# Attention with squared ReLU and a gated feed-forward on one core: swaps of normalised x two head pairs at a time, two loads moved up, the last tile's copies on VectorE

## The chip, the cores and the metric

The kernel runs on one core of a Trainium2 chip. The metric is the device time of one execution in microseconds (us). Before the change the median of six runs is 444.49 us, with 442.97 as the lowest and 447.28 as the highest.

## The reference

Attention over 8 batches, 12 heads, 448 positions and a head dimension of 64, whose scores go through a squared ReLU in place of a softmax; then, on the 3584 tokens of width 768, an RMS norm and a gated feed-forward of width 1536.

```python
scores = scale * np.matmul(q, k.transpose(0, 1, 3, 2))
attn = np.maximum(scores, 0.0) ** 2 / S
attn_out = np.matmul(attn, v)
x = attn_out.transpose(0, 2, 1, 3).reshape(B * S, H * D)
xn = x / np.sqrt(np.mean(x * x, axis=-1, keepdims=True) + 1e-06) * rms_g
g, val = xn @ w_gate, xn @ w_val
out = (g / (1 + np.exp(-g)) * val) @ w_out
```

## The kernel before

Two heads make a head pair, 128 rows of x transposed; a batch has six pairs (`HP` = `KT` = 6) and 448 columns. Everything runs in an order written out by hand: `weave(main, sides)` (line 17) interleaves a list of main units (feed-forward matmuls) with side steps (the attention of the next batch, loads, transposes), each side step having a position in the list. Each engine and each issuing queue works through its own instructions in that order.

Per batch b these stages follow each other:

- `fetch(b)` (line 88) loads q, k and v on POOL's queue, casting to bf16. Two buffers each hold the batches in turn.
- `trans_fill(b, half)` (line 677), for batches from 2 on: two DMA transposes on SP's queue (`transposes`, lines 163 and 167) make qT and kT of six heads, then two copies on POOL's queue (`fill`, lines 175 and 176) copy the halves of qT across the partitions. Batches 0 and 1 are transposed by TensorE instead (`pe_transposes`, line 128).
- Scores (lines 187, 207 and 228), ReLU on ScalarE or VectorE, squares on VectorE or ScalarE, the product with v (`attend`, line 273), and `leave` (line 288), which writes the pair's rows into xT on ScalarE.
- `norm_stat` (line 437) sums the squares over the rows on TensorE and takes the root and its reciprocal, `norm_spread` (line 476) spreads it over the partitions into rstd, and `norm_apply` (line 491) multiplies xT by it, pair by pair, on VectorE (line 500). For batches from 2 on it also issues the swaps.
- `swap` (line 339) makes xD, which is xT with its partition halves exchanged. Each swap is two DMAs on SP's queue (line 342), one for each half. It is needed because each matmul of the feed-forward uses 64 partitions: the upper half of the array multiplies by the gate weights, the lower by the value weights, and every head has to pass both.
- `gate_value(b)` (line 605): 12 blocks of 12 rounds each. A round (`rounds`, line 512) is one matmul for gate (psG) and one for value (psV) with one pair: six rounds over xT and six over xD, in order of the pairs. The order of the half blocks is such that the first two blocks' rounds over xT come before the first round over xD. Then silu on ScalarE (line 564) and the product into hT on VectorE (line 566).
- `out_tiles` (line 614): 128 tokens of two batches at a time, in a piece of 512 and a piece of 256 columns, each over the 12 row blocks of `wo_sb` (line 435). ScalarE copies the piece from PSUM (line 586), and `store` (line 592) issues the writes on SP's queue; those of the very last tile go on SP's and ScalarE's queues, and its second piece is cut in two of 128 columns.

At the start the loads stand on POOL's queue in the order q, k, v of batch 0, then slices of the gate and value weights with q, k and v of batch 1 between them, then six slices of w_out (`fetch_o`, line 117, each two row blocks of `wo_sb`), then q, k, v of batch 2 (line 743), then the fills of batch 2 (line 744). The attention of batch 0 is a list of units (`attention_first`, line 347), with pairs of matmuls on a constant tile between them (`warm`, line 656). Its end is written out (lines 707 to 738): single rounds of batch 0's feed-forward on x not yet normalised (`part`, line 703, the round numbers 0 to 5 over xT and 6 to 11, from `KT` on, over xD) are put between its last units and its norm. These first three blocks (psE) are copied out by ScalarE (`early_out`, line 532) and scaled later. SP's queue carries all the swaps, transposes and stores in one order.

Of the kernel before, what the change touches and what calls it, by code (L numbers as in the profile page):

```python
# [29 lines left out]
def along(p0, gap, fns):  # L30
    return [(p0 + gap * i, f) for i, f in enumerate(fns)]
# [3 lines left out]
def kernel(  # L35
# [11 lines left out]
    nc = tc.nc  # L47
    P = nc.NUM_PARTITIONS
    B, H, S, D = q.shape
# [4 lines left out]
    KT, FT, HP = DM // P, F // P, H // 2  # L54
# [3 lines left out]
    NT = 2 * S // P  # L58
# [20 lines left out]
    def head_rows(t, b, h0, h1):  # L79
        return t[b, h0:h1].rearrange("h (p c) d -> p h (c d)", c=NCH)  # L80
# [3 lines left out]
    def alloc_ld(b):  # L84
        for nm in ("q", "k", "v"):
            ld[nm, b] = ldpool.tile([PC, H, NCH * D], BF16, name=nm + "b", tag=nm + "b", bufs=2)

    def fetch(b):
        alloc_ld(b)
        for nm in ("q", "k", "v"):  # L90
            load(nm, b)

    def load(nm, b, h0=0, h1=H):
        src = {"q": q, "k": k, "v": v}[nm]
        return nc.gpsimd.dma_start(out=ld[nm, b][:, h0:h1, :], in_=head_rows(src, b, h0, h1))
# [13 lines left out]
    def fetch_gv(s):  # L109
        for prt, src in gv_slices(s * FS, (s + 1) * FS):  # L110
            last = nc.gpsimd.dma_start(out=wgv_sb[prt, :, s * FS : (s + 1) * FS], in_=src)
        return last

    def wo_rows(t, s):
        return t.rearrange("(fk p) m -> p fk m", p=P)[:, 2 * s : 2 * s + 2, :]

    def fetch_o(s):
        return nc.gpsimd.dma_start(out=wo_sb[:, 2 * s : 2 * s + 2, :], in_=wo_rows(moe_w_out, s))
# [37 lines left out]
    def transposes(b, half):  # L156

        hs = slice(half * HH, (half + 1) * HH)  # L160
        kT = late["kT"].tile([P, HH, 2, PC], BF16, name="kT", tag="kT")
        qT = late["kT"].tile([P, 3, HH, 2, PC], BF16, name="qT", tag="qT")
        nc.sync.dma_start_transpose(
            out=qT[:, 1].rearrange("p h c s -> p (h c) s"),
            in_=ld["q", b][:, hs, :].rearrange("p h m -> p (h m)"),
        )
        nc.sync.dma_start_transpose(
            out=kT[:].rearrange("p h c s -> p (h c) s"),
            in_=ld["k", b][:, hs, :].rearrange("p h m -> p (h m)"),
        )  # L170
        kqT[b, half] = (kT, qT)

    def fill(b, half, eng):
        qT = kqT[b, half][1]
        eng.dma_start(out=qT[:HALF, 2], in_=qT[HALF:, 1])  # L175
        eng.dma_start(out=qT[HALF:, 0], in_=qT[:HALF, 1])
# [156 lines left out]
    def cross(b, j, psAV):  # L333

        low, high = slice(0, HALF), slice(HALF, P)
        for to, fr in ((low, high), (high, low)):
            nc.scalar.mul(out=xDs[b][to, j, :], in_=psAV[fr, 0, :], mul=ga_sb[fr, j : j + 1])

    def swap(b, j0, j1, eng=None):

        for hf in (0, 1):
            (eng or nc.sync).dma_start(
                out=xDs[b][hf * HALF : (hf + 1) * HALF, j0:j1, :],
                in_=xTs[b][(1 - hf) * HALF : (2 - hf) * HALF, j0:j1, :],
            )
# [85 lines left out]
    def halves(ps, w, lhsT, rhs, start, stop):  # L431

        for hf in range(2):
            prt = slice(hf * HALF, (hf + 1) * HALF)
            nc.tensor.matmul(out=ps[prt, :w], lhsT=lhsT[:, prt], rhs=rhs, start=start, stop=stop)  # L435
# [55 lines left out]
    def norm_apply(b):  # L491


        raws = [xTs[b]] + ([xDs[b]] if b < 2 else [])
        if b == 0:
            xTs[b] = npool.tile([P, KT, S], BF16, name="xT", tag="xT", bufs=2)
            xDs[b] = npool.tile([P, KT, S], BF16, name="xD", tag="xD", bufs=2)
        for raw_x, x in zip(raws, (xTs[b], xDs[b])):
            for kt in range(KT):
                nc.vector.tensor_tensor(  # L500
                    out=x[:, kt, :], in0=raw_x[:, kt, :], in1=rstds[b][:], op=ALU.mult
                )
                if b > 1 and kt % 3 == 2:
                    swap(b, kt - 2, kt + 1)

    def hidden(b):
        i = b // 2
# [60 lines left out]
    osts = {}  # L568
# [8 lines left out]
    def out_piece(i, t, o, w):  # L577
        ps = ps_m.tile([P, 512], FP32, name="psO", tag="mm")
        for fk in range(FT):
            halves(  # L580
                ps, w, hTs[i][:, fk, t * P : (t + 1) * P], wo_sb[:, fk, o : o + w],
                fk == 0, fk == FT - 1,
            )
        if o == 0:
            osts[i, t] = late["ost"].tile([P, DM], FP32, name="ost", tag="ost")
        nc.scalar.copy(out=osts[i, t][:, o : o + w], in_=ps[:, :w])  # L586
        if (i, t) == (B // 2 - 1, NT - 1):
            store(i, t, o, o + w, (nc.sync, nc.scalar))
        elif o + w == DM:
            store(i, t, 0, DM, (nc.sync, nc.sync))  # L590

    def store(i, t, c0, c1, engs):
        g, end, k = t * P, (t + 1) * P, 0
        while g < end:
            n = min(end, (g // PC + 1) * PC) - g
            b, c, p0 = 2 * i + g // S, g % S // PC, g % PC
            c = c if b < 2 else (0, 2, 1, 3)[c]
            rows = out[b * S : (b + 1) * S, :].rearrange("(p u) m -> p u m", u=NCH)
            engs[k % 2].dma_start(
                out=rows[p0 : p0 + n, c, c0:c1],  # L600
                in_=osts[i, t][g - t * P : g - t * P + n, c0:c1],
            )
            g, k = g + n, k + 1
# [52 lines left out]
    def warm(n):  # L656

        ps = ps_m.tile([P, S], FP32, name="psW", tag="mm")
        for _ in range(n):
            nc.tensor.matmul(out=ps[:], lhsT=warm_in[:, :P], rhs=warm_in[:], start=True, stop=True)  # L660
# [8 lines left out]
    load("v", 1)  # L669
    for s in range(4, NSL):  # L670
        fetch_gv(s)
    for s in range(FT // 2):
        fetch_o(s)
    late["kT"] = pool("kT", 2)
    EB = 3
# [1 line left out]
    def trans_fill(b, half):  # L677
        transposes(b, half)
        fill(b, half, nc.gpsimd)

    with tc.tile_pool(name="qkT", bufs=2, side="right") as tp, tc.tile_pool(
        name="early", bufs=EB, side="right"
    ) as ep:
        late["qkT"], late["early"] = tp, ep
        warm(12)
        steps = attention_second(1)

        def early_block(fb):
            return [ps_m.tile([P, S], FP32, name="psE", tag="mm")[:] for _ in range(2)]

        units = attention_first(0)
        tail = len(units) - 4
        for n, fn in enumerate(units[:tail]):
            fn()
            if n % 3 == 2:
                warm(2)


        raw_x = xTs[0], xDs[0]
        psSS = ps_m.tile([P, S], FP32, name="psSS", tag="mm")  # L700
        blocks = [early_block(0)]

        def part(fb, *rs):
            for r in rs:
                rounds(0, fb, blocks[fb], r, r + 1, raw_x)

        psAV4 = psAVs[0, (HP - 2,)]
        squares_last, leave_4, attend_5, leave_5 = units[tail:]
        squares_last()
        part(0, 0, 1)  # L710
        pe_transposes(1, 0)
        leave_4()
        attend_5()
        leave_5()
        cross(0, HP - 2, psAV4)
        part(0, 2, 3, KT, HP - 2)
        norm_stat(0, psSS, steps.pop(0))
        part(0, KT + 1, KT + 2)
        norm_spread(0)
        blocks.append(early_block(1))  # L720
        part(1, *range(KT))
        part(0, HP - 1)
        part(1, *range(KT, KT + 3))
        part(0, KT + 4)
        steps.pop(0)()
        part(1, KT + 4)
        norm_apply(0)
        for fb in range(2):
            part(fb, KT + 3, KT + 5)
            early_out(0, fb, blocks[fb])  # L730
            if fb == 0:
                pe_transposes(1, 1)
        for fb in range(2, EB):
            blocks.append(early_block(fb))
            for r0 in range(0, 2 * KT, KT):
                steps.pop(0)()
                rounds(0, fb, blocks[fb], r0, r0 + KT, raw_x)
            early_out(0, fb, blocks[fb])
        main = gate_value(0, EB, KT // 2)
        sides = along(6.4, 2, [lambda fb=fb: early_scale(0, fb) for fb in range(EB)])  # L740
        sides += along(10.4, 2, [lambda fb=fb: early_rest(0, fb) for fb in range(EB)])
        sides += along(0, (len(main) - 1) / len(steps), steps[:-1])
        sides += [(18.2, lambda: fetch(2))]
        sides += [(28, lambda: trans_fill(2, 0))]
        weave(main, sides)
    late["ost"] = pool("ostage", 3)
    late["sum"] = pool("sum")
# [7 lines left out]
    for b in range(1, B):  # L755
# [5 lines left out]
        sides = []  # L761
# [39 lines left out]
```

## Time and profile before

| what | value |
|---|---|
| median of 6 runs | 444.49 us |
| the profiled execution | 445.35 us |
| its span, first to last instruction | 443.5 us |
| granted TensorE clock | 1.00 |
| mean data rate of the DMAs | 120 GB/s |
| packets of q0 (POOL's loads and fills) | 43.3% of 16 engines' span |
| packets of q1 (SP's queue) | 29.1% of 16 engines' span |

The span of the profiled execution lies within its time; what is in the time and not in the span are 1.9 us around it. A row of the page's fifth part has the line, the engine, the operation, what it writes and reads, the number of instructions, the busy time and the mean of one in ns, and then how long the engine sat idle before them. For the work around the change:

```profile
L242 ACT ACTIVATE r<-psS 112x896 bf16<-112x896 f32 x108 | 99.1, 918 | 22.2 <-PE psS L228 19.4
L435 PE MATMUL psO<-wo_sb,hT 128*64 128x512 bf16 (+2 forms) x1368 | 111.8, 323 | 0.0
L500 DVE TENSOR_TENSOR xT<-xT,rstd 128x448 bf16<-128x448 bf16 x48 | 26.4, 618 | 2.1 <-ACT rstd L488 2.1
```

And the DMA issues of the loads that move, with the size of one and the median time from issue to landing:

```profile
qb<-in_q_dram POOLq DMA_DIRECT2D x6, 672.0 KB, 12.2
kb<-in_k_dram POOLq DMA_DIRECT2D x6, 672.0 KB, 14.7
wo_sb<-in_moe_w_out_dram POOLq DMA_DIRECT2D x6, 384.0 KB, 16.3
xD<-xT SPq DMA_DIRECT2D x24, 168.0 KB, 2.7
```

In the timeline, one row is one instruction or several alike, with its start, its length, and in brackets how long its engine sat idle before it and what ended that. POOLq, SPq and ACTq are the queues' own instructions, such as DMA issues.

### The profile page before, as it was taken

Reading aid. Unit: us, or ns where it says so; the run is one execution under the profiler, and the core shown is the slowest. Engines: PE = TensorE matmul, PEld = TensorE weight load, DVE = VectorE, ACT = ScalarE, POOL = GpSimd, SP = SyncE. Lnnn points to the kernel's source line nnn. Section 1 sums busy time; section 2 is a strip of 40 time slices with the busy share of each in tenths; the row PEclk is TensorE's granted clock in tenths of the full one; section 3 lists DMA queues with packets and bytes.
Section 4 is the critical chain, followed back from the end, with each engine's and each line's share of the span. In section 5 each row is a group of like instructions: output and inputs, shape, how many; then the busy total and the mean of one; then the engine's idle time right before and its main releaser. Section 6 shows DMA issues by size and latency. Waiting matters only on the chain.

```text
span 443.5 us, 10907 instructions
## 1 busy us (share of the span) xinstructions
PE 433.3 (98%) x4720; PEld 249.5 (56%) x4720; DVE 287.7 (65%) x384; ACT 288.8 (65%) x448; POOL 53.7 (12%) x79
## 2 busy tenths in 40 slices
PE   7999999899999999999999999999999999999996
PEld 3345555655566545655566555665557555655664
DVE  4989985766853868666874668578676468742210
ACT  4899886577674775866755776666766667552221
POOL 8343300030000300021000300003000000000000
PEclk9999999999999999999999999999999999999999
DMA  9999999999216992179904997179912900041013
GB/s 130 196 201 198 200 215 193 150 198 171 58 37 133 192 167 57 37 179 168 148 18 111 190 201 81 35 121 185 170 37 68 227 7 1 1 120 51 1 37 109
DMA packets 86673, 53.21 MB, mean 120 GB/s; under 512 B 36577, under 2 KB 80737, under 8 KB 86625
## 3 DMA queue, kind: packets, MB, share of 16 engines
q0 software_dynamic: 44496, 27.50, 43.3%
q1 hardware_dynamic: 41504, 24.44, 29.1%
q8 instruction: 37, 0.61, 0.6%
q10 hardware_dynamic: 624, 0.57, 0.4%
q14 instruction: 12, 0.09, 0.1%
HBM read 47.19 MB, written 11.01 MB: 131 GB/s over the span
## 4 chain that ended last, share of the span: by engine, by line
PE 70%; DMA 19%; DVE 4%; ACT 2%; POOL 1%; issue 1%; SPq 0%; ACTq 0%; POOLq 0%
PE psG L520 26%; PE psO L435 18%; PE psV L520 13%; PE psAV L273 6%; PE psS L228 6%; DMA qb<-in_q_dram 4%; DMA kb<-in_k_dram 4%; DMA wgv_sb<-in_moe_w_gate_dram 4%; DMA qT<-qb 3%; DMA vb<-in_v_dram 2%; DVE xT L500 1%; DMA xD<-xT 1%; DVE r L240 1%; DMA qT<-qT 1%; DVE hT L566 1%
## 5 line engine op out<-in xcount | busy, mean ns | idle before, releaser
L520 PEld LDWEIGHTS <-wgv_sb 64*128 64x128 bf16 x2304 | 126.0, 94 | 96.1 <-issue 7.6
L520 PE MATMUL psG<-xT,wgv_sb 64*128 64x448 bf16 x558 | 128.7, 349 | 0.0
L520 PE MATMUL psV<-xD,wgv_sb 64*128 64x448 bf16 x558 | 128.4, 349 | 0.2 <-DMA xD<-xT 0.2
L520 PE MATMUL psG<-xD,wgv_sb 64*128 64x448 bf16 x558 | 128.4, 349 | 0.1
L520 PE MATMUL psV<-xT,wgv_sb 64*128 64x448 bf16 x558 | 128.0, 349 | 0.1
L242 ACT ACTIVATE r<-psS 112x896 bf16<-112x896 f32 x108 | 99.1, 918 | 22.2 <-PE psS L228 19.4
L435 PE MATMUL psO<-wo_sb,hT 128*64 128x512 bf16 (+2 forms) x1368 | 111.8, 323 | 0.0
L566 DVE TENSOR_TENSOR hT<-sil,psV 128x448 bf16<-128x448 bf16 x93 | 57.4, 617 | 62.7 <-ACT sil L564 62.6
L246 DVE TENSOR_TENSOR r<-r 112x1792 bf16<-112x1792 bf16 x72 | 78.0, 1088 | 30.8 <-ACT r L242 30.4
L435 PEld LDWEIGHTS <-hT 128*64 128x64 bf16 x1368 | 74.8, 110 | 35.7 <-issue 0.4
L564 ACT ACTIVATE sil<-psG 128x448 bf16<-128x448 f32 x93 | 50.5, 543 | 58.4 <-PE psV L520 34.6
L228 PE MATMUL psS<-qT,kT 64*128 64x448 bf16 (+1 forms) x288 | 57.1, 350 | 1.7 <-DMA qT<-qT 1.3
L586 ACT COPY ost<-psO 128x512 f32<-128x512 f32 (+2 forms) x57 | 26.2, 471 | 42.9 <-PE psO L435 42.5
L240 DVE TENSOR_SCALAR r<-psS 112x896 bf16<-112x896 f32 x36 | 39.0, 1084 | 2.0 <-PE psS L228 1.8
L273 PE MATMUL psAV<-r,vb 112*64 112x448 bf16 x384 | 40.3, 355 | 0.0
L175 POOL DMA_DIRECT2D qT<-qT x12 | 6.5, 541 | 264.7 <-PE psS L228 139.0
L273 PEld LDWEIGHTS <-vb 112*64 112x64 bf16 x384 | 20.1, 109 | 18.5 <-issue 6.5
L329 ACT ACTIVATE xT<-psAV,ga_sb 128x448 bf16<-128x448 f32 x47 | 27.8, 647 | 3.9 <-PE psAV L273 3.8
L228 PEld LDWEIGHTS <-kT 64*128 64x128 bf16 (+1 forms) x288 | 19.3, 97 | 16.1 <-issue 5.2
L500 DVE TENSOR_TENSOR xT<-xT,rstd 128x448 bf16<-128x448 bf16 x48 | 26.4, 618 | 2.1 <-ACT rstd L488 2.1
L471 DVE RECIPROCAL rhalf<-rhalf 128x224 f32<-128x224 f32 x8 | 12.4, 1553 | 21.3 <-ACT rhalf L465 21.3
L256 DVE TENSOR_TENSOR r<-r 112x1792 bf16<-112x1792 bf16 x23 | 24.3, 1083 | 0.7 <-ACT r L217 0.7
(67 smaller groups left out, 279.0 us busy)
## 6 DMA issues: line engine op xcount, KB each, us to landing
vb<-in_v_dram POOLq DMA_DIRECT2D x7, 672.0 KB, 18.7
qb<-in_q_dram POOLq DMA_DIRECT2D x6, 672.0 KB, 12.2
kb<-in_k_dram POOLq DMA_DIRECT2D x6, 672.0 KB, 14.7
qT<-qT POOLq DMA_DIRECT2D x24, 168.0 KB, 3.9
xD<-xT SPq DMA_DIRECT2D x24, 168.0 KB, 2.7
out_dram<-ost SPq DMA_DIRECT2D x7, 336.0 KB, 4.0
wgv_sb<-in_moe_w_gate_dram POOLq DMA_DIRECT2D x6, 384.0 KB, 16.3
wgv_sb<-in_moe_w_val_dram POOLq DMA_DIRECT2D x6, 384.0 KB, 16.7
```

The source lines that it names most:

```text
L228: nc.tensor.matmul(out=psS[: end - o, hf, :S], lhsT=flat[prt, o:end], rhs=qT[prt, 1 - hf : 3 - hf, h % HH], start=True, stop=True,)
L240: nc.vector.tensor_relu(out=r[:, cp], in_=src)
L242: nc.scalar.activation(out=r[:, cp], in_=src, func=ACT.Relu)
L246: nc.vector.tensor_tensor(out=r[:], in0=r[:], in1=r[:], op=ALU.mult)
L273: nc.tensor.matmul(out=part[hh * D : (hh + 1) * D, :], lhsT=ld["v", b][:, 2 * j + hh, c * D : (c + 1) * D], rhs=rsq[b, 2 * j + hh, c], sta ...
L329: nc.scalar.mul(out=xTs[b][:, j, :], in_=psAV[:, i, :], mul=ga_sb[:, j : j + 1])
L435: nc.tensor.matmul(out=ps[prt, :w], lhsT=lhsT[:, prt], rhs=rhs, start=start, stop=stop)
L500: nc.vector.tensor_tensor(out=x[:, kt, :], in0=raw_x[:, kt, :], in1=rstds[b][:], op=ALU.mult)
L520: nc.tensor.matmul(out=parts[part][:, :S], lhsT=wgv_sb[prt, h, fb * P : (fb + 1) * P], rhs=src[prt, kt, :], start=(r == 0), stop=(r == 2 * ...
L564: nc.scalar.activation(out=s[:], in_=psG, func=ACT.Silu)
L566: nc.vector.tensor_tensor(out=hT[:, fb, o : o + S], in0=s[:], in1=psV, op=ALU.mult)
L586: nc.scalar.copy(out=osts[i, t][:, o : o + w], in_=ps[:, :w])
```

## The change

Four edits:

1. In `norm_apply`, for batches from 2 on, the swaps are issued after every second pair instead of every third: three swaps (six DMAs of 112 KB) in place of two (four of 168 KB).
2. The copies of the very last output tile (pieces of 512, 128 and 128 columns) are done by VectorE instead of ScalarE. Their stores stay on SP's and ScalarE's queues.
3. Of the six slices of w_out only four stay ahead of the loads of batch 2. q and k of batch 2 follow them, then the other two slices, then the fills of half 0, then v. `trans_fill(2, 0)` stands at position 26 of the woven list instead of 28; on SP's queue this doesn't change the order.
4. At the end of batch 0's attention the last pair of warm-up matmuls is left out; rounds 2 and 3 move ahead of the transposes of batch 1, and rounds 7 and 8 (`KT + 1`, `KT + 2`) ahead of the norm's sums.

```diff
-                if b > 1 and kt % 3 == 2:
-                    swap(b, kt - 2, kt + 1)
+                if b > 1 and kt % 2:
+                    swap(b, kt - 1, kt + 1)
...
-        nc.scalar.copy(out=osts[i, t][:, o : o + w], in_=ps[:, :w])
-        if (i, t) == (B // 2 - 1, NT - 1):
+        last = (i, t) == (B // 2 - 1, NT - 1)
+        (nc.vector.tensor_copy if last else nc.scalar.copy)(
+            out=osts[i, t][:, o : o + w], in_=ps[:, :w]
+        )
+        if last:
             store(i, t, o, o + w, (nc.sync, nc.scalar))
...
-    for s in range(FT // 2):
+    for s in range(4):
         fetch_o(s)
...
         for n, fn in enumerate(units[:tail]):
             fn()
-            if n % 3 == 2:
+            if n % 3 == 2 and n < tail - 1:
                 warm(2)
...
         squares_last()
-        part(0, 0, 1)
+        part(0, *range(HP - 2))
         pe_transposes(1, 0)
...
         cross(0, HP - 2, psAV4)
-        part(0, 2, 3, KT, HP - 2)
+        part(0, KT, HP - 2, KT + 1, KT + 2)
         norm_stat(0, psSS, steps.pop(0))
-        part(0, KT + 1, KT + 2)
         norm_spread(0)
...
-        sides += [(18.2, lambda: fetch(2))]
-        sides += [(28, lambda: trans_fill(2, 0))]
+        sides += [(26, lambda: trans_fill(2, 0))]
+        alloc_ld(2)
+        load("q", 2)
+        load("k", 2)
+        for s in range(4, FT // 2):
+            fetch_o(s)
+        sides += [(26, lambda: load("v", 2))]
         weave(main, sides)
```

## The prediction

> **What bounds the kernel now.** I read the page's busy times first, then equal stretches of TensorE's work side by side, then the chain of waits where a stretch is longer than its twins.
>
> ```profile
> PE 433.3 (98%) x4720; PEld 249.5 (56%) x4720; DVE 287.7 (65%) x384; ACT 288.8 (65%) x448; POOL 53.7 (12%) x79
> ```
>
> TensorE is busy for 98% of the 443.5 us, at a granted clock of 1.00. An edit can thus take out a pause of TensorE, work of TensorE, or the start and end of the kernel; relief elsewhere is worth nothing. A busy TensorE may still issue late, so I compared stretches with the same 146 matmuls: from the first score of a batch's main stage (L228) to its first value product (L273), for batches 1, 2, 3 and 5. The first column is the stretch and its length, the next TensorE's busy time.
>
> ```profile
> 86.96:102.56 15.60, 14.31 (x146) 8.07 (x144) 11.28 (x15) 10.48 (x14) 3.90 (x5) 1.00 1.07 183
> 141.66:155.57 13.91, 13.91 (x146) 7.50 (x144) 9.58 (x11) 10.42 (x14) 3.91 (x5) 1.00 1.04 195
> 190.77:205.30 14.53, 14.41 (x146) 7.75 (x144) 9.58 (x11) 10.42 (x14) 3.90 (x5) 1.00 0.93 191
> 293.51:307.42 13.91, 13.91 (x146) 7.50 (x144) 9.58 (x11) 10.42 (x14) 3.90 (x5) 1.00 1.03 193
> ```
>
> 13.91 us is the undisturbed length (batches 4 and 6 have it too). Batch 1 loses 15.60 - 13.91 = 1.69 us, batch 3 loses 0.62. Batch 7 computes no scores; there one round stands 0.50 us from the one before where 0.19 is usual, which is 0.31 us, and with the unevenness behind it about 0.45. The cause in batch 1, from the timeline and the chain:
>
> ```profile
> 86.96 0.36 PE L228 MATMUL psS<-qT,kT 64*128 64x448 bf16 x1
> 88.61 0.35 PE L228 MATMUL psS<-qT,kT 64*128 64x448 bf16 x1 [1.29 <-DMA qT<-qT]
> ```
>
> ```profile
> 52.37 17.95 DMA qb<-in_q_dram
> ...
> 70.34 11.27 DMA qT<-qb
> ...
> 82.22 0.54 POOL qT L175
> 82.76 5.81 DMA qT<-qT
> ...
> 88.61 0.35 PE psS L228
> ```
>
> Four transfers in a row: load of q of batch 2, its transpose, the fill of the other half, and only then the second score matmul. In batch 3 the chain runs over the swap of normalised x:
>
> ```profile
> 187.43 3.31 DVE xT L500 x6
> 190.76 0.46 SPq L342
> 191.26 3.51 DMA xD<-xT
> 194.81 0.35 PE psV L520
> ```
>
> **The change, part by part.** All is deducted from the median of 444.49 us. The profiled execution took 445.35 us for a span of 443.5, so 1.9 us lie around the span; it is 0.86 above the median, so its stalls may be a little longer than usual.
>
> *Loads.* On POOL's queue the order becomes wo 0 to 3, q2, k2, wo 4 and 5, the two fills of half 0, v2; before it was wo 0 to 5, q2, k2, v2, fills. q2 moves up two places: from 52.37 to about the 48.43 at which wo 4 was issued. Two slices of wo are 768 KB; the transfers moved some 205 GB/s around 50 to 60 us, so q2 lands 3.8 us earlier, at 66.5. The transpose on SP's queue stands behind the swap of batch 1 that is issued at 67.04 for 1.10 us, so it starts at 68.2 instead of 70.34. With the old landing of 11.27 us it ends at 79.4, with the median of the qT transposes, 7.7, at 75.9. The fills then issue 0.6 and 1.15 us later, and with 5.81 (old) or 3.9 us (median) the second lands at 86.4 or 80.9. TensorE asks at 86.96. The 1.69 us go. k2 moves likewise, its transpose from 74.61 to about 70.8, so the swap behind it on SP (78.19 now, its xT ready at 76.0) comes sooner too. Bounds: nothing (the fill is as late as before) to 1.69. What is late next: wo 4 and 5, which now take the bytes' place of k2 and v2. As many bytes lie ahead of wo 5 as lay ahead of k2, which landed 20.2 us after 54.44, at 74.6:
>
> ```profile
> qb<-in_q_dram POOLq DMA_DIRECT2D x1, 672.0 KB, 18.0
> kb<-in_k_dram POOLq DMA_DIRECT2D x1, 672.0 KB, 20.2
> vb<-in_v_dram POOLq DMA_DIRECT2D x1, 672.0 KB, 23.7
> ```
>
> The first output tile starts at 74.59 and takes 2.59 us for its 12 rows of wo, so wo 5 (the last two) is wanted at 76.7. v2's tail beside the transposes shows what contention may add: 672 KB at 200 GB/s behind k2 would have landed at 78.0, and landed at 80.0. So wo 5 lands at 74.6 to 76.6: covered, barely. v2, now behind the fills on POOL, is issued at 77.5 to 81.1 and wanted at 102.56 - 1.69 = 100.9. Behind it on POOL wait the fills of half 1 (issued at 90.28) and the loads of batch 3; v2's issue costs them 0.95 us, and the half-1 fill is wanted only after the value product at 102.56.
>
> *Start of batch 0's tail.* One pair of warm-up matmuls goes (0.37 us of TensorE), two rounds (of 0.19 us) move ahead of the transposes and two ahead of the norm's sums. This gives nothing, because ScalarE sets the pace there: 7.88 and 8.00 us busy in the 8 us from 30 and from 38, and TensorE waits for it to empty a PSUM tile:
>
> ```profile
> 37.61 0.94 ACT L532 COPY gv<-psE 128x448 f32<-128x448 f32 x2
> 38.18 0.79 PE L520 MATMUL psE<-xT,wgv_sb 64*128 64x448 bf16 x3
> ```
>
> What TensorE saves before 38.18 it waits there. If that cover failed I would gain 0.37. The moved rounds read xD of pair 2, whose second swap is issued at 25.10; swaps there land in 5.8 to 6.1 us, so at 31.2, wanted at about 31.9. If it came late, the norm's sum (32.22 to 32.99) has 0.33 us before ScalarE takes it. Bounds 0 to 0.37 gain; taken 0.
>
> *Swaps in twos.* Six transfers of 112 KB instead of four of 168 KB in each of six norms. SP spends 0.46 to 0.60 us on each, so the first starts after two multiplies (188.58, not 189.16), and two still follow the last multiply at 190.74: at about 190.9 and 191.4, the latter 0.15 later than now. What TensorE stalled on, pair 3, leaves in the middle swap, issued 1 us earlier; pair 4 is wanted 0.19 us after it, at 194.38. Cautiously, the last swap lands after the old 3.51 us less 56 KB at the 237 GB/s of 191.2 to 193.2 (0.24 us): 194.68, a stall of 0.30 instead of 0.62. In batch 7 the same reckoning gives 396.26 + 2.81 - 0.24 = 398.83 against 398.67, a stall of 0.16 instead of 0.45. At best, since the data starts to move 0.6 us sooner, both stalls go: 1.07. At worst the size matters nothing and only the 0.19 of the later want counts, less 0.15: 0.04 a place, 0.1 in all. I take 0.8, between the cautious 0.6 and the best. The transposes queued behind on SP are delayed by the 0.15 us and have many us in hand; in batches 2, 4 and 6 the swaps are not waited for.
>
> The Trainium skill speaks against this edit: "DMA: Bandwidth & Descriptors", section on the anatomy of one DMA, puts about 2.0 us fixed on every transfer and only bytes / 436 GB/s on top, so that 112 KB would land merely 0.13 us before 168 KB; by that this part would be worth about 0.4 us. The rule is fitted on loads that GpSimd issues, the swaps leave SP. The trace, where 168 KB landed in 2.8 to 3.5 us, agrees with a large fixed share; it doesn't separate the two.
>
> *Last tile.* Its three copies go from ScalarE to VectorE, which is idle then.
>
> ```profile
> 439.51 0.38 ACTq L599 DMA_DIRECT2D out_dram<-ost  x1
> 439.93 0.27 ACT L586 COPY ost<-psO 128x128 f32<-128x128 f32 x1 [0.45 <-ACT ost L586]
> 440.30 0.33 ACTq L599 DMA_DIRECT2D out_dram<-ost  x1
> ```
>
> The last matmul starts at 439.21 and takes 0.22, but the copy waits until 439.93 for ScalarE, which is issuing a store. VectorE would start at 439.46. Its price for 128 f32 columns from PSUM isn't in the trace: 0.16 us by proportion from its 224-column f32 copy (282 ns), 0.40 by the line through its PSUM reads of 448 and 896 columns (684 and 1084 ns); I take 0.28, the nearest row. The store then issues at 439.79, not 440.30: 0.51 less (0.39 to 0.57, since ScalarE's queue is busy with the second store until about 439.7).
>
> Sum: 1.69 + 0 + 0.8 + 0.51 = 3.0 us; 444.49 - 3.0 = 441.5.
>
> **The rivals.** *The swaps in twos bring nothing* (0.1 instead of 0.8): 444.49 - 1.69 - 0.1 - 0.51 = 442.2. For it: the last swap starts no earlier. Against it: the late pair is no longer in the last swap. *The wait at 86.96 only moves*: wo 5 lands late at 76.7, or the fill does: 444.49 - 0.8 - 0.51 = 443.2. For it: the margins of 0.1 and 0.56 us at the far ends. Against it: the near ends leave 2 and 6 us. *Slower: v2 comes too late.* It moved from 56.34 to behind the fills; at the far end 81.1 plus the longest landing of a vb load, 23.7, is 104.8, a wait of 3.9 us at L273, so 444.49 - 3.0 + 3.9 = 445.4. It decides from a landing after 103.9. Against it: those 23.7 us stood behind two slices of wo, q2 and k2, and the shortest vb load took 7.6.
>
> **How the numbers follow.** Forecast 0.62 (440.8 to 442.2 with its own bounds), swaps nothing 0.14, the wait moves 0.15, slower 0.09. About 0.5%, 2.2 us, is what a measurement of this kernel can tell from no change: faster is below 442.27, slower above 446.71. Nine tenths of the forecast and half of the first rival are faster, 0.63; beyond 446.71 v2 must land after 106, past all rows, 0.07; the rest is the same, 0.30. The range runs from the forecast's best with TensorE's 0.37 (440.4) to the second rival with a late pair of wo (444.2), which leaves out the slower one.
>
> **What would show it.** Right: the stretch of batch 1 is 13.91 us long; no wait for qT or xD; transposes at 68; the last store issues at 439.8 less what came before; TensorE's pause at 38 grows by some 0.37. Wrong: an output tile at 76 that waits for wo, a first value product that waits for vb, a stretch of batch 3 still at 14.5, or ScalarE moving ahead before 38.

## The result, and the profile after

The changed kernel takes 443.21 us as the median of 33 runs (442.32 to 443.95), the kernel before 444.38 us as the median of its 70 runs now (442.74 to 448.16). The ratio is 0.9973, with a 95% interval of 0.9963 to 0.9983: 1.17 us faster, less than half of the 3.0 us forecast, and by the prediction's own bound of 0.5% no change. The time lies in the range (440.4 to 444.2). The runs also lie closer together: 8 in 10 of them between 442.67 and 443.81, before between 443.14 and 445.67.

The profiled execution took 442.98 us for a span of 441.2, at a granted clock of 1.00; before it was 445.35 us for 443.5. The two profiled executions thus differ by 2.4 us where the medians differ by 1.2, and a comparison of the two profiles alone would find twice the gain that the times show. Of the 2.4 us, 0.40 lie ahead of the first value product, at 13.01 us before and 12.61 after; in the thirteen traces read here it comes at 12.31 to 13.02 us, whatever the edit. First the busy times, from the first part of the page of the changed kernel:

```profile
PE 432.0 (98%) x4718; PEld 248.8 (56%) x4718; DVE 288.8 (65%) x387; ACT 287.6 (65%) x445; POOL 53.9 (12%) x79
```

Two matmuls and three ScalarE copies fewer, three VectorE copies more; the other instruction counts in this row are the same. Then the same stretches as in the prediction, from the first score to the first value product of batches 1, 2, 3 and 5 (columns: stretch and length, then TensorE's busy time and others):

```profile
86.43:100.41 13.98, 13.98 (x146) 7.49 (x145) 11.29 (x15) 10.40 (x14) 3.89 (x5) 1.00 1.01 187
139.50:153.42 13.92, 13.92 (x147) 7.52 (x145) 9.58 (x11) 10.42 (x14) 3.92 (x5) 1.00 1.08 211
188.61:203.26 14.65, 14.28 (x147) 7.71 (x146) 9.70 (x11) 10.40 (x14) 3.91 (x5) 1.00 0.85 179
291.48:305.39 13.91, 13.91 (x146) 7.51 (x144) 9.58 (x11) 10.42 (x14) 3.90 (x5) 1.00 0.95 186
```

Batch 1's stretch went from 15.60 to 13.98, the undisturbed length. Batch 3's did not get better: 14.65, against 14.53 before. In the timeline of the changed kernel the loads, fills, transposes and swaps in front of batch 1's stretch now stand as follows, first POOL's queue and then SP's (start, length, line, operation, and what ended the idle time before it):

```profile
48.21 0.96 POOL L95 DMA_DIRECT2D qb<-in_q_dram  x1 [1.60 <-ACT r L217]
50.17 0.94 POOL L95 DMA_DIRECT2D kb<-in_k_dram  x1 [1.01 <-DVE hT L566]
51.95 0.71 POOL L118 DMA_DIRECT2D wo_sb<-in_moe_w_out_dram  x1 [0.83 <-DMA wgv_sb<-in_moe_w_gate_dram]
54.94 0.71 POOL L118 DMA_DIRECT2D wo_sb<-in_moe_w_out_dram  x1 [2.28 <-DMA wgv_sb<-in_moe_w_val_dram]
75.54 0.56 POOL L175 DMA_DIRECT2D qT<-qT  x1 [19.89 <-DMA qT<-qb]
76.09 0.55 POOL L176 DMA_DIRECT2D qT<-qT  x1
76.62 0.99 POOL L95 DMA_DIRECT2D vb<-in_v_dram  x1
```

```profile
67.65 1.53 SPq L163 DMA_TRANSPOSE qT<-qb  x1
69.23 4.83 SPq L167 DMA_TRANSPOSE kT<-kb  x1
75.44 1.83 SPq L342 DMA_DIRECT2D xD<-xT  x2
```

q of batch 2 is issued at 48.21 instead of 52.37, its transpose starts at 67.65 instead of 70.34, and the fill is issued at 75.54, eleven microseconds before the first score. In the list of TensorE's waits there is none for qT any more; for the swaps there still is:

```profile
PE psV L520 <- DMA xD<-xT: 0.3, 1, 0.3
```

### The profile page after: what moved, and what is told of

It reads as the page before. It is cut to its first block, busy times and chain, and to the rows that moved or that the text cites. A ratio compares the mean times of both kernels' runs of the same rounds, so it can differ in the third digit from the quotient of the medians.

```text
span 441.2 us, 10928 instructions
## 1 busy us (share of the span) xinstructions
PE 432.0 (98%) x4718; PEld 248.8 (56%) x4718; DVE 288.8 (65%) x387; ACT 287.6 (65%) x445; POOL 53.9 (12%) x79
## 4 chain that ended last, share of the span: by engine, by line
PE 86%; ACT 7%; DVE 4%; issue 1%; DMA 1%; SPq 0%; ACTq 0%; DVEq 0%
PE psG L520 30%; PE psO L435 23%; PE psV L520 13%; PE psAV L273 9%; PE psS L228 6%; ACT r L217 2%; PE psW L663 2%; DVE r L240 1%; PE psS L187 1%; ACT r L197 1%; ACT sil L564 1%; DVE hT L566 1%; DMA xD<-xT 1%; DVE xT L500 1%; PE psT L143 1%
## 5 line engine op out<-in xcount | busy, mean ns | idle before, releaser
L228 PE MATMUL psS<-qT,kT 64*128 64x448 bf16 (+1 forms) x288 | 56.1, 350 | 0.4
L587 ACT COPY ost<-psO 128x512 f32<-128x512 f32 (+1 forms) x54 | 25.1, 477 | 39.8 <-PE psO L435 39.8
```

Source lines behind the costliest of these rows:

```text
L228: nc.tensor.matmul(out=psS[: end - o, hf, :S], lhsT=flat[prt, o:end], rhs=qT[prt, 1 - hf : 3 - hf, h % HH], start=True, stop=True,)
L587: (nc.vector.tensor_copy if last else nc.scalar.copy)(out=osts[i, t][:, o : o + w], in_=ps[:, :w])
```

## The experiments

All ratios are against the kernel before on the same chip. The runs came on three chips, whose medians of the kernel before were 443.86, 443.99 and 444.87 us; runs of one chip are compared with each other.

### Each edit by itself

First chip, four kernels: the kernel before with one edit of the change each. In the cuts of code, `...` stands for lines left out. The loads:

```diff
-    for s in range(FT // 2):
+    for s in range(4):
         fetch_o(s)
...
-        sides += [(18.2, lambda: fetch(2))]
-        sides += [(28, lambda: trans_fill(2, 0))]
+        sides += [(26, lambda: trans_fill(2, 0))]
+        alloc_ld(2)
+        load("q", 2)
...
+        sides += [(26, lambda: load("v", 2))]
```

> The kernel before with the new order of loads alone (edit 3). Theory A, the whole gain of 1.17 us comes from this edit: ratio to before near 0.9975 (1.0 to 1.3 us faster), narrower spread of times than before (before: 442.7 to 448.2), batch 1's stretch 13.9 to 14.0 us instead of 15.60. Rival B, this edit gives the full 1.69 us that the profiled execution of before lost and another edit gives 0.5 back: ratio near 0.9962.

The swaps:

```diff
-                if b > 1 and kt % 3 == 2:
-                    swap(b, kt - 2, kt + 1)
+                if b > 1 and kt % 2:
+                    swap(b, kt - 1, kt + 1)
```

> The kernel before with the swaps in twos alone (edit 1). Theory A, a swap lands some 3.4 us after its issue whatever its size, so nothing is won: ratio 0.999 to 1.001, batch 3's stretch still 14.5 to 14.7 us, batch 7 still with a wait of 0.1 to 0.5 us. Rival B, the two more issues cost time: ratio 1.001 or more. The prediction's own figure was 0.8 us faster, 0.9982.

The last tile:

```diff
+        last = (i, t) == (B // 2 - 1, NT - 1)
-        nc.scalar.copy(out=osts[i, t][:, o : o + w], in_=ps[:, :w])
+        (nc.vector.tensor_copy if last else nc.scalar.copy)(
+            out=osts[i, t][:, o : o + w], in_=ps[:, :w]
+        )
```

> The kernel before with the last tile's copies on VectorE alone (edit 2). Theory A, the copies are earlier but the stores, now back to back on two queues, take longer to issue (0.85 and 1.03 us for the second pair in the changed kernel instead of 0.37): 0.1 to 0.2 us faster, ratio 0.9996, the last store issued about 1.3 us after the last matmul's start. If the stretched issue was chance: 0.5 us faster, ratio 0.9989, the last store 0.6 us after. Rival B: slower, 1.0005 or more.

The start:

```diff
-            if n % 3 == 2:
+            if n % 3 == 2 and n < tail - 1:
                 warm(2)
...
-        part(0, 0, 1)
+        part(0, *range(HP - 2))
...
-        part(0, 2, 3, KT, HP - 2)
+        part(0, KT, HP - 2, KT + 1, KT + 2)
         norm_stat(0, psSS, steps.pop(0))
-        part(0, KT + 1, KT + 2)
```

> The kernel before without the last warm-up pair and with the rounds moved (edit 4). Theory A, ScalarE sets the pace at 28 to 38 us: ratio 0.9995 to 1.0005, and TensorE's first block after the pause at 38 starts at the same distance from ScalarE's copy. If TensorE's saving came through: 0.37 us faster, 0.9992. Rival B, this edit costs time: 1.0005 or more.

| edit alone | median us | ratio, 95% interval | profiled us |
|---|---|---|---|
| loads | 443.71 | 0.9984 [0.9963, 1.0005] | 443.78 |
| swaps | 444.66 | 1.0012 [0.9990, 1.0035] | 444.68 |
| last tile | 443.95 | 0.9996 [0.9980, 1.0012] | 444.61 |
| start | 444.91 | 1.0016 [0.9993, 1.0039] | 447.14 |

No interval excludes 1. By the ratio the loads bring 0.7 us (by the medians 0.15) and the others nothing that shows, so the times alone settle little here; the traces have to do it.

The loads do in the trace what was expected. From the value products ahead of the first output tile to the next ones, 29.51 us before (73.05 to 102.56), it is 27.90 with the loads alone and in six of the seven other traces with the new order that are read here; the seventh, with 28.59, is told below. With the old order it is never below 28.91.

The start edit's trace shows 39.35 us from the first value product (about 13 us) to the one at 52, as the traces of the loads, the swaps and the last tile alone do (39.35 or 39.36), and 39.51 before, 39.37 after. It is worth nothing that shows. Its long profiled time has another cause, and that is the old order of the loads at its worst. From the chain of waits of the kernel with the start edit alone (start, length, what; `...` stands for lines left out):

```profile
57.34 17.48 DMA qb<-in_q_dram
74.84 8.59 DMA qT<-qb
...
84.57 4.66 DMA qT<-qT
89.27 0.35 PE psS L228
```

q of batch 2 was issued at 57.34 there, 5 us later than in the trace of before, and the stretch from 73 took 30.60 us. The load's place in POOL's queue is the same in both. What held POOL isn't settled: it sits idle for some microseconds before each load, and the releaser named differs from run to run. Nor does the issue alone set the loss: with the swaps alone q of batch 2 was issued at 54.42 and 1.01 us were lost, before at 52.37 and 1.61, since there the transfers behind it took longer (transpose 11.27 us and second fill 5.81, against 10.87 and 4.57).

So the old order's loss varies from one execution to the next, and the traces of five kernels that have it show how (the loss is the stretch less 27.90; beside it, how far the profiled execution lies above the median of its kernel's runs):

| kernel with the old order | loss us | profiled less median us |
|---|---|---|
| swaps alone | 1.01 | 0.02 |
| before | 1.61 | 0.97 |
| changed, old loads (below) | 1.66 | 1.06 |
| last tile alone | 1.72 | 0.66 |
| start alone | 2.70 | 2.23 |

The execution that took the median time lost 1.0 us; the others lost more, and were longer by nearly as much. The five lie 1.0 us above their medians on average. In seven traces with the new order the profiled execution lies 0.5 us below to 0.8 us above, on average at the median; an eighth, told below, lay 1.2 above.

### The change less one edit, and two variants of it

Second chip. The changed kernel with swaps in threes again:

```diff
-                if b > 1 and kt % 2:
-                    swap(b, kt - 1, kt + 1)
+                if b > 1 and kt % 3 == 2:
+                    swap(b, kt - 2, kt + 1)
```

> The changed kernel with the swaps in threes again (edit 1 undone, edits 2 to 4 kept). Theory A, a swap in twos is worth only the 0.2 us that batch 7 showed: median within 0.3 us of the changed kernel's, batch 3's stretch 14.3 to 14.8 us, the last stage (first matmul of batch 7 to its first output matmul) 27.97 us instead of 27.80. Prediction's figure, 0.8 us for the swaps: about 0.8 us slower than the changed kernel.

The changed kernel with ScalarE's copies at the end again:

```diff
-        (nc.vector.tensor_copy if last else nc.scalar.copy)(
+        nc.scalar.copy(
```

> The changed kernel with the last tile's copies on ScalarE again (edit 2 undone). Theory A, the store issues set the end, and their length varies (0.38 to 1.12 us for the second one over four executions with ScalarE): 0.1 to 0.4 us slower than the changed kernel, last store issued 1.1 to 1.8 us after the start of the last matmul. Prediction's figure: 0.5 us slower.

The changed kernel with the last piece of 256 columns whole:

```diff
-        if (i, t, o) == (B // 2 - 1, NT - 1, 512):
-            for o, w in ((o, w // 2), (o + w // 2, w // 2)):
-                out_piece(i, t, o, w)
-            return
```

> The changed kernel with the last tile's second piece whole, 256 columns in one copy and two stores instead of two copies and four stores. Theory A, the second pair of stores holds up the third, so leaving it out brings the last store to about 0.7 us after the start of the last matmul (a copy of some 0.42 us after its 0.22) instead of 1.0 to 1.3: 0.3 to 0.6 us faster than the changed kernel, ratio to before near 0.9963. Rival, the end is set by the size of the last copy and the landing of a store: 0.1 us faster to 0.2 us slower than the changed kernel.

And a test of what the swaps' time hangs on. In batches 3, 5 and 7 the pairs 3 to 5 are swapped before the norm, as soon as their rows are in xT, and VectorE multiplies their xD as well; pairs 0 to 2 are swapped together after three multiplies, and the other batches' swaps go in threes:

```diff
             leave(b, (j, j + 1))
+            if b % 2 and j:
+                swap(b, max(j, 3), j + 2)
...
+        early_x = b > 1 and b % 2
+        if early_x:
+            raws.append(xDs[b])
...
+                if early_x:
+                    if n == 0 and kt == 2:
+                        swap(b, 0, 3)
+                elif b > 1 and kt % 3 == 2:
+                    swap(b, kt - 2, kt + 1)
```

> The changed kernel, but for batches 3, 5 and 7 the pairs 3 to 5 are swapped before the norm, and their xD is then multiplied on VectorE (three more multiplies of 0.62 us a batch); pairs 0 to 2 go in one swap after three multiplies; batches 2, 4 and 6 swap in threes. Theory A, what TensorE waits for is the time from a swap's issue to its landing, 2.3 to 3.6 us whatever its size, after the last multiplies: with those swaps out of the way batch 3's stretch falls from 14.65 to 13.9 us and the last stage from 27.80 to about 27.5: 0.7 to 1.0 us faster than the changed kernel. Rival, VectorE becomes the bound in these stages: the stretches of batches 3 and 5 grow beyond 14.0 and nothing is won.

| changed kernel with | median us | ratio, 95% interval | profiled us |
|---|---|---|---|
| swaps in threes | 443.65 | 0.9992 [0.9979, 1.0006] | 444.87 |
| ScalarE's copies | 443.65 | 0.9988 [0.9975, 1.0001] | 443.70 |
| last piece whole | 443.07 | 0.9976 [0.9964, 0.9988] | 442.54 |
| swaps before the norm | 442.67 | 0.9967 [0.9954, 0.9979] | 442.82 |

*Swaps.* In batch 3's stretch, undisturbed 13.91 us, five traces with swaps in threes show 14.32 to 15.31 (mean 14.80), and six with swaps in twos 14.45 to 14.74 (mean 14.62). From the first matmul of batch 7's feed-forward to the first of its output tiles, swaps in threes show 27.95 to 28.02 us and swaps in twos 27.72 to 27.81: 0.22 less. By the traces swaps in twos thus bring some 0.4 us in all: the 0.22 in batch 7, where the two groups lie apart, and 0.18 in batch 3, where they overlap. Why so little is in the chain of waits of the changed kernel around batch 3's norm:

```profile
185.91 2.67 DVE xT L500 x5
...
188.64 0.58 SPq L342
...
189.32 0.55 SPq L342
189.86 0.05 issue
189.92 3.35 DMA xD<-xT
193.27 0.04 issue
193.31 0.35 PE psV L520
```

The last of the six swaps carries 112 KB and lands 3.35 us after it is issued, at 193.27; before, 168 KB took 3.51. The multiplies end at 188.58 (185.91 + 2.67), so this last transfer is issued 1.34 us after them; before, with one pair of DMAs less, it was 0.52 (191.26 against 190.74). SP's queue is behind: the trace has its six issues at 186.47, 186.98, 188.10, 188.64, 189.32 and 189.92, and the third stands 0.59 us after its pairs were multiplied (187.51), in batch 5 only 0.17. What it waited for in batch 3 isn't settled, but it isn't chance: in all six traces with swaps in twos it is 0.57 to 0.59 us. The later ones have to queue behind it; even in batch 5 the last swap is issued 0.98 us after the multiplies' end. TensorE stops twice on the way, for the middle pairs and for the last ones (from the timeline):

```profile
191.84 0.35 PE L520 MATMUL psG<-xD,wgv_sb 64*128 64x448 bf16 x1
192.29 0.35 PE L520 MATMUL psV<-xD,wgv_sb 64*128 64x448 bf16 x1
...
192.69 0.35 PE L520 MATMUL psG<-xD,wgv_sb 64*128 64x448 bf16 x1
193.31 0.35 PE L520 MATMUL psV<-xD,wgv_sb 64*128 64x448 bf16 x1 [0.27 <-DMA xD<-xT]
```

A round usually follows the one before by 0.19 us, here by 0.45 and 0.62: 0.26 and 0.43 us lost, 0.69 of the 0.74.

The long landings go with something that the chain doesn't name. Among the DMA queues the page of the changed kernel lists one whose kind is "instruction":

```profile
q8 instruction: 37, 0.61, 0.5%
```

Each of its 37 packets carries 16 KB. The trace has their times: in batch 3 one runs from 189.86 to 190.95, while the last four swaps are under way; in batch 5, which doesn't stall, none runs while the swaps do. In the eleven traces whose swaps are all in twos or all in threes, batches 2 to 7, this parts the landings:

| swaps | no such packet in the first 2.6 us after the issue | with one |
|---|---|---|
| 112 KB | 152 landed after 2.12 to 2.44 us, median 2.23 | 64 after 2.17 to 4.19, median 3.33 |
| 168 KB | 83 landed after 2.53 to 3.09 us, median 2.61 | 37 after 2.51 to 4.38, median 3.42 |

So the smaller size lands some 0.4 us sooner, and a packet of q8 beside a swap goes with about 1 us more, whatever the size. That the packet delays the swap is read from this; no edit moved the packets, and whose instructions they carry isn't shown. In batch 7 no such packet runs beside the last swaps, and there the two effects of the edit can be seen bare: the last swap lands after 2.33 us instead of 2.81, and is issued 1.01 us after the last multiply instead of 0.53. They cancel. What is left is that the last swap now holds pairs 4 and 5, which are wanted 0.19 us later than pair 3.

With the swaps of three pairs before the norm, the same stretch and that of batch 5 are:

```profile
189.00:202.92 13.92, 13.92 (x147) 7.52 (x146) 11.16 (x14) 10.42 (x14) 3.88 (x5) 1.00 1.03 184
291.13:305.05 13.92, 13.92 (x148) 7.53 (x146) 11.16 (x15) 10.42 (x14) 3.89 (x5) 1.00 0.98 190
```

No wait for xD is left on TensorE's list, although VectorE has three multiplies more there (11.16 us busy instead of 9.70 in batch 3). In this trace the wait has thus gone. Two things differ at once, though: half of the pairs were swapped early, and batch 3's packet of q8 begins at 190.89, after the last swap has landed (190.68).

*Last tile.* VectorE's copies start when the matmuls end and the last one takes 0.29 us. But the stores don't follow. From the timeline of the changed kernel, the last matmuls, VectorE's last copy, and the second and third stores on ScalarE's queue (four views):

```profile
437.01 0.22 PE L435 MATMUL psO<-wo_sb,hT 128*64 128x128 bf16 x2
437.27 0.29 DVE L587 COPY ost<-psO 128x128 f32<-128x128 f32 x1 [0.38 <-PE psO L435]
437.18 1.03 ACTq L602 DMA_DIRECT2D out_dram<-ost  x1
438.30 0.39 ACTq L602 DMA_DIRECT2D out_dram<-ost  x1
```

The last copy ends at 437.56, and its store is issued at 438.30, since the store before it kept the queue for 1.03 us. Before, that one took 0.38. From the last matmul's start to the last store's issue, five traces with ScalarE's copies show 1.09, 1.17, 1.28, 1.33 and 1.81 us (mean 1.34; the 1.09 is the trace that the prediction was made on), six with VectorE's 1.02 to 1.39 (mean 1.25); to the end of the span it is 4.59 and 4.31 us in the mean, and both pairs of ranges overlap. So the edit brings 0.1 to 0.3 us by these means. With the last piece whole there is a store less on each queue, and in that kernel's timeline

```profile
436.61 0.28 PE L435 MATMUL psO<-wo_sb,hT 128*64 128x256 bf16 x2
437.38 0.37 ACTq L598 DMA_DIRECT2D out_dram<-ost  x1
```

the last store is issued 0.77 us after the last matmul's start, and its issue takes 0.37.

What held the second stores can be read from the traces too: again it goes with a packet of q8. The table has start and end, in us, of the last packet of q8 and of the issues of the second store on each queue.

| kernel | packet of q8 | issue on SP's queue | on ScalarE's queue |
|---|---|---|---|
| before | 438.55 to 439.51 | 439.51 to 439.88 | 439.51 to 439.89 |
| loads alone | 436.44 to 437.71 | 437.18 to 438.07 | 437.18 to 438.30 |
| last tile alone | 437.88 to 439.07 | 438.64 to 439.43 | 438.71 to 439.46 |
| changed | 436.45 to 437.61 | 437.12 to 437.97 | 437.18 to 438.21 |
| last piece whole | 441.83 to 442.79 | 437.38 to 437.69 | 437.38 to 437.76 |

In all eleven traces that have the packet there, the issue on SP's queue ends 0.35 to 0.37 us after the packet does, and that on ScalarE's 0.37 to 0.60. In the trace of before the packet ended just as these issues began, and they took no longer than others (0.37 and 0.38 us). That the issues wait for the packet is read from this; no edit moved the packet alone. In the two kernels with the last piece whole the packet comes after the last instruction, and the issues are short (0.31 and 0.37 or 0.38).

*A wait that appeared.* The kernel with swaps in threes has its profiled time 1.2 us above its median, and TensorE's list of waits says why:

```profile
PE psG L520 <- DMA xD<-xT: 0.6, 1, 0.6
PE psO L435 <- DMA wo_sb<-in_moe_w_out_dram: 0.5, 1, 0.5
```

The last slice of w_out was issued at 57.84 there, against 54.94 in the changed kernel's trace, and landed at about 77.2; the first output tile took 3.25 us instead of 2.59. This is the second rival's thin margin, seen in one of eight traces with the new order.

### The two best together, the change again, and its loads undone

Third chip. Swaps before the norm and the last piece whole, the two edits just shown, on top of the change:

> The changed kernel with both edits that won: pairs 3 to 5 of batches 3, 5 and 7 swapped before the norm, and the last tile's second piece whole. Theory A, the two add up, since one is at 190 and 396 us and the other at the end: 0.7 to 1.1 us faster than the changed kernel of the same call, ratio to before near 0.9960. Rival, they don't add: no faster than the kernel with the earlier swaps alone, 0.9967.

The changed kernel itself, with no edit:

> The changed kernel itself, on the same chip as the others of this call and as a second profile of it. Theory A: ratio to before 0.997 to 0.998, batch 1's stretch 13.9 to 14.0 us, batch 3's 14.5 to 14.8, last stage 27.7 to 27.8.

The changed kernel with the old order of the loads:

```diff
-    for s in range(4):
+    for s in range(FT // 2):
...
-        sides += [(26, lambda: trans_fill(2, 0))]
-        alloc_ld(2)
...
-        sides += [(26, lambda: load("v", 2))]
+        sides += [(18.2, lambda: fetch(2))]
+        sides += [(28, lambda: trans_fill(2, 0))]
```

> The changed kernel with the old order of loads (edit 3 undone, the rest kept). Theory A, the loads carry most of the gain, and in a timed execution the wait is smaller than in a profiled one: median 0.5 to 1.0 us above the changed kernel's of this call, with a wider spread; in the profile 1.0 to 2.7 us are lost between 73 us and batch 1's first value product. Rival B, the full 1.69 us are lost in timed executions too.

The changed kernel with v of batch 2 ahead of the fills on POOL's queue:

```diff
-        sides += [(26, lambda: load("v", 2))]
+        sides += [(25, lambda: load("v", 2))]
```

> The changed kernel with v of batch 2 loaded ahead of the fills instead of behind them; q and k keep their place before the last two slices of w_out. Theory A, it is q's earlier landing that pays and v's place hardly matters: the same as the changed kernel within 0.3 us, batch 1's stretch 13.9 to 14.0. Rival, v's bytes beside the transposes are what made the fill late: a wait for qT at batch 1's first scores is back, 0.3 us or more slower.

| kernel | median us | ratio, 95% interval | profiled us |
|---|---|---|---|
| both together | 443.62 | 0.9981 [0.9966, 0.9995] | 444.38 |
| changed | 443.16 | 0.9964 [0.9950, 0.9978] | 442.88 |
| changed, old loads | 443.81 | 0.9995 [0.9974, 1.0016] | 444.87 |
| changed, v ahead of the fills | 443.56 | 0.9979 [0.9954, 1.0004] | not read |

The old loads cost the changed kernel 0.65 us in the median (1.0 in the mean, 1.4 by the two ratios), and spread its runs from 443.09 to 447.31 where they lay between 442.63 and 443.51. The stretch of batch 1 is back at its old length in the trace:

```profile
86.54:102.18 15.64, 14.31 (x146) 8.08 (x144) 11.37 (x15) 10.47 (x14) 3.90 (x5) 1.00 1.10 189
```

Both together were not faster than the change alone. The spans, from the first instruction to the last, say otherwise: their median is 440.85 us with both edits and 441.4 for the changed kernel, 0.55 less. What grew is the time around the span: 1.86 to 3.67 us in the twelve runs, 1.72 to 1.90 for the changed kernel. The last piece whole, alone, shows a little of it (1.83 to 2.15); no other kernel here has more than 1.95. These two kernels are also the only ones whose last packet of q8 comes after the last instruction (443.25 to 444.62 in the trace with both edits, whose span ends at 441.32). That the end waits for it fits, but wasn't tested.

In the trace with both edits batch 3's stretch is 14.43, and the chain of waits shows a swap of 168 KB that was issued at 187.94 and took 4.41 us:

```profile
187.94 4.41 DMA xD<-xT
192.39 0.35 PE psV L528
```

Here the first of these swaps on SP stood at 187.41, and at 187.39 in the kernel with swaps before the norm that had no wait. What differs is the packet of q8: it came at 190.06, with the swap still under way, and not at 190.89. So even those swaps aren't safe. Whether that version beats the changed kernel stays open: on the second chip it was the fastest by 0.4 us or more, but the changed kernel wasn't run beside it there. The place of v can't be told from the change (0.4 us, with overlapping intervals); the profiled execution of that kernel took 902 us, so there is no trace to compare, and whether batch 1's wait came back in it isn't known.

## Why the prediction was right in direction and wrong in size

**Loads: the mechanism right, the term too large.** Each step came as written: transpose at 67.65 (68.2 was forecast), wait for qT gone, stretch at 13.98. But the term was 1.69 us, taken in full from the profiled execution and deducted from the median of 444.49. The prediction noted that this execution lay 0.86 above the median and that its stalls "may be a little longer than usual", and then left the term as it was. The experiments give 0.7 (loads alone, by the ratio, with an interval that holds 0; 0.15 by the medians) and 0.65 (loads undone, by the medians; 1.4 by the ratios). The trace whose time was at the median lost 1.0. The step that failed is taking one execution's stall for that of the median. This is the largest error, some 0.7 to 1.0 of the 1.8 us too many.

**Swaps in twos: the first rival was nearer.** 0.8 was forecast; the traces give 0.2 in batch 7, near the 0.29 reckoned there (a stall of 0.16 instead of 0.45; the kernels without a wait there take 27.65 us, so the whole stall was 0.34), and about 0.2 in batch 3, where 0.32 was reckoned and 0.7 still stalls. Two steps failed. The last transfer was to be issued 0.15 us later than before (191.4 against 191.26, by multiplies that end at 190.74) and went 0.82 later, reckoned from the multiplies' end (1.34 against 0.52), in batch 7 0.48 later. And the landing was to go from 3.51 us to 3.27 with the size: undisturbed the size gains even more, some 0.4 us, but the 3.51 wasn't a matter of size. A packet of q8 ran beside the swap (191.84 to 192.87 before), another after (189.86 to 190.95), and the landing is 3.35. The packets of q8 are the cost that the prediction left out. Of the signs of being wrong that it named one came, and it is this: batch 3's stretch, still at 14.65. The rule of the Trainium skill ("DMA: Bandwidth & Descriptors", section on the anatomy of one DMA), about 2.0 us fixed and from its rate an estimated difference of 0.13 us between the two sizes, would by the prediction's reckoning have made this part 0.4, as the runs have it. That is luck: without a packet of q8 the two sizes differ by 0.38 us in the traces (2.61 and 2.23), not 0.13, and the 0.16 of batch 3 compares two disturbed landings.

**Last tile: the copy right, the queue behind it wrong.** The copies take what the prediction took (0.29 us for 128 columns, 0.28 forecast; the 512 columns take 0.69). The prediction reckoned the second store's issue at 0.38 us, as in the trace of before, and said that its queue is busy until about 439.7. It took 1.03. All six traces with VectorE's copies have 0.75 to 1.12 us there, the five with ScalarE's 0.38 to 1.12, most of them 0.5 to 0.6. So 0.51 became 0.1 to 0.3. The 0.38 was luck: the trace that the prediction was made on is the one in which the packet of q8 ended as the issue began. In the other ten traces that have a packet there, the issues end soon after it whichever engine copies (on SP's queue 0.35 to 0.37 us), so an earlier copy gains little. That the stores now come closer together (0.47 us from the first to the second instead of 0.71) doesn't explain it: with the loads alone 0.71 us lie between, and the issue takes 1.12.

**Start: nothing, as forecast.** ScalarE sets the pace there; four traces, three without the edit and one with it, agree to 0.01 us. TensorE resumes 0.56 us after ScalarE's copy of psE begins (37.64 and 37.08), as before (38.18 and 37.61).

**Rivals.** The wait for wo is real but rare (one trace of eight). v of batch 2 was issued at 76.62 in the changed kernel's trace, a little ahead of the range given (77.5 to 81.1), and no trace shows TensorE waiting for it; the slower case did not come.

The parts as measured, 0.65 to 1.0 for the loads, some 0.4 for the swaps and 0.1 to 0.3 for the last tile, add to 1.15 to 1.7; measured were 1.17. Within the spread of the parts the gain is accounted for, and the changed kernel's trace shows no new wait of TensorE; what failed is the size of all three terms.

## What to carry to other kernels

A stall whose length depends on when a load lands differs from one execution to the next; take it from an execution whose time is the median, or deduct from the stall what the profiled execution lies above the median. Cutting a small transfer smaller shortens its landing, but adds issues to the queue, and in batch 7 the two cancelled; issue it earlier instead. Where one of several like stages stalls and its twins don't, look among the DMA packets for what is only there; here it was a packet of the instruction queue. When a copy at the end moves to another engine, look at the queue that issues its store: it may be the next to wait.

## What the runs showed of the hardware

The issue of one DMA on ScalarE's or SP's queue is not a fixed price: the same store took 0.38 to 1.12 us to issue, and a swap in the middle of the kernel 1.42 us (189.92 to 191.34) where the others there took 0.47 to 0.60. That issue, too, ended 0.39 us after a packet of q8 (190.95). A transfer of 168 KB between the partition halves, 2.61 us in the median when no such packet came beside it, took up to 4.41 us to land with one. And a load with the same place in POOL's queue was issued between 52.37 and 57.34 us, a delay that the old order can turn into time and the new one mostly doesn't. That fits with the changed kernel's runs lying within 1.6 us of each other and those before within 5.4.
